# Moving the operand sums of x and u through the routing rounds of a spectral + PEER kernel (1 core)

## The chip, the cores and the metric

One core of one Trainium2 chip runs the kernel. The metric is the device time of one execution in microseconds (us): the median of three runs, each of which is the slowest core's time (there is one core here).

## The reference

For 2048 tokens of width 512, `y = x + FNet(xn) + PEER(xn)`, where `xn` is the layer norm of `x`:

```python
y = einsum("ts,bse->bte", re_s, xn @ re_d.T) - einsum("ts,bse->bte", im_s, xn @ im_d.T)   # real part of a 2-D DFT
q = einsum("nd,dhc->nhc", xf, w_q)             # 32 heads, two halves of 128
s1, s2 = q[..., :128] . k1, q[..., 128:] . k2  # 64 scores each; the best two of each half
cand = t1[..., :, None] + t2[..., None, :]     # 4 candidates of which the best two remain, out of 4096 experts
g = softmax(top_s)
act = gelu(einsum("nd,nhkd->nhk", xf, u[top_e]))
out = einsum("nhk,nhk,nhkd->nd", g, act, v[top_e])
```

The kernel doesn't gather experts: it computes `x @ u.T` for all 4096 of them, multiplies by the gates that the routing gives, and multiplies the product by `v`.

## The kernel before, in words

**Start (0 to about 96 us).** Loads, the layer norm, the transforms of the spectral part.

**Routing (to about 480 us).** Eight rounds `j` of four heads each, over 16 token tiles `i`; "tile n" below is number `16*j + i`. For each tile `scores` lets PE do 12 matmuls of 128x512 into one of four PSUM banks (L252), ACT copy the bank to one of four buffers `ss` (L949), and DVE find the best two per head (eight MAX8, L953, two FIND_INDEX8, L957). A bank comes free when ACT has copied it. A round's weights `m` are made during the round before: `m_prep` scales the raw weights (ACT L162; the scaled raw copy on ACT, L164, for parts t = 2 and 3, on POOL, L166, for t = 0 and 1) and takes the difference (POOL, L167), and `m_mul` multiplies them on PE (L148). `routing` turns the best two of each half into gates, early in the next round (lines 882 to 922, on POOL, DVE and ACT; L887 on POOL is what ACT's L890 takes). `y_rows` (PE L528 to L531, POOL L540 and L541) finishes rows of the spectral part during rounds 0 to 2.

Other work is spread among the tiles by `todo[n]`, a list of pieces for each tile, and each is tied to its tile by `behind()` (L737): ACT copies the piece's scale factor into a spare column of the tile's `ss` buffer, and the piece reads it from there. So a piece can't start before that `ss` buffer is in use for tile n. The pieces are:

- `fill_uv` (ACT L780 and L781, POOL L782): splits a block of `u` or `v` into two f16 halves in SBUF, 16 blocks of u and 9 of v.
- `sum_u`: for the eight blocks of u that belong to QUADS, four sums on POOL (L808 to L811), then `split4`, ACT's f16 copy of them (L794), POOL's difference (L795), and two stores to DRAM (`s_d`, L798).
- `sum_x`: the same for the six token pairs in PAIRS: one large sum (POOL L821), four small ones (L826 to L829), the same `split4`, two stores to `t_d` (L798). Its pieces stand at `todo[62 + 7n]` and just behind, but nothing in them is tied to the tile: `sum_x` takes no scale factor.
- `stage_v` (ACT L846 and L847, POOL L849): as a fill, but stored to DRAM.

All `sum_u` share one scratch buffer (`v_sb[8]`) and half of `v_sb[6]`, all `sum_x` share `v_sb[5]`, `v_sb[7]` and the other half of `v_sb[6]`; each next one waits until the store of the last has read them. A scheduler reorders the queue of each engine as data allow, so that the six `sum_x` without a tie stand in POOL's queue ahead of work of round 0.

**Products (from about 480 us).** PE computes `z = x @ u.T`, ACT takes gelu, PE expands the gates (L1241), DVE multiplies, PE multiplies by v (L1286). For six pairs of token tiles the products with the eight QUADS blocks follow a Strassen-like scheme (`z_pair`): seven products per quad (`slot`, L1153, 24 matmuls of 128x128), four of them with summed u (`s_d`, loaded at L1136 into a ring of three buffers) and some with summed x (`t_d`). `SEQ` gives the order: a digit is a product, a and b are the two quads, c is an ordinary block (24 matmuls of 128x256, L1092) out of PLAIN, the eight blocks outside QUADS. Products 5, 6, 3 and 7 read the ring; when one has been issued, `ring_load` refills its buffer. Gate expansions (L1241) are put between by a count of PE cycles done. The gelu of a quad writes its four blocks with a stride that `dst` gives.

Of the kernel before, what the change touches and what calls it, by code (L numbers as in the profile page):

```python
# [20 lines left out]
D = 512  # L21
# [7 lines left out]
XS = 512.0  # L29
V1 = 5  # L30
V2 = 9
QUADS = (0, 1, 2, 3), (8, 9, 10, 11)
PAIRS = tuple(range(2, 14, 2))


# [1 line left out]
def tile_fnet_peer(ctx, tc, x, ca, cb, c5, wt, wf, wr, wq, kt, ut, vn, out):  # L37
# [117 lines left out]
    def m_prep(j, t, pool, at):  # L155

        raw = MS[j, t].rearrange("p h k -> p (h k)")
        MS[j, t, "h"] = pool.tile([P, 2, D], F16, tag="wh", name=f"wh{j}_{t}", bufs=4)
        h = MS[j, t, "h"].rearrange("p h k -> p (h k)")
        l = raw.bitcast(F16)[:, 0:2 * D]  # L160
        MS[j, t, "l"] = l.rearrange("p (h k) -> p h k", h=2)
        nc.scalar.activation(h, raw, AF.Copy, scale=at)  # L162
        if t > 1:
            nc.scalar.activation(raw, raw, AF.Copy, scale=at)  # L164
        else:
            nc.gpsimd.tensor_scalar(raw, raw, sw, None, op0=ALU.mult)  # L166
        nc.gpsimd.tensor_tensor(l, raw, h, op=ALU.subtract)  # L167
# [553 lines left out]
    def part_b(safe, stS, stP, stQ, stE, xt, u_sb, cmp_p, w4):  # L721
# [11 lines left out]
        def behind(src, at):  # L733

            if at is None:
                return src
            nc.scalar.activation(at, src, AF.Copy)  # L737
            return at
# [48 lines left out]
        def scratch(g):  # L787
            return v_sb[g].rearrange("p l c d -> p (l c d)").bitcast(F32)
# [24 lines left out]
            split4(part - 1, s4, v_sb[6].rearrange("p l c d -> p (l c d)")[:, 0:2 * D],  # L813
                   lambda i: s_d[qd].rearrange("o p (t l f) -> t l p o f", t=4, l=2)[t, i])

        def sum_x(b, part):

            f, t4 = scratch(5), scratch(7)
            if part == 0:
                v = xq[b // 2]  # L820
                nc.gpsimd.tensor_tensor(f.rearrange("p (q f) -> p q f", q=2),  # L821
                                        v[:, :, 0].rearrange("p q k n -> p q (k n)"),
                                        v[:, :, 1].rearrange("p q k n -> p q (k n)"), op=ALU.add)
                b11, b21, b12, b22 = [f[:, k * 256:k * 256 + 256] for k in range(4)]
                r = [t4[:, k * 256:k * 256 + 256] for k in range(4)]
                nc.gpsimd.tensor_tensor(r[0], b12, b11, op=ALU.subtract)  # L826
                nc.gpsimd.tensor_tensor(r[1], b22, r[0], op=ALU.subtract)
                nc.gpsimd.tensor_tensor(r[2], b22, b12, op=ALU.subtract)
                nc.gpsimd.tensor_tensor(r[3], b21, r[1], op=ALU.subtract)  # L829
                return  # L830
            split4(part - 1, t4, v_sb[6].rearrange("p l c d -> p (l c d)")[:, 2 * D:],
                   lambda i: t_d[b // 2, :, i * 2 * D:i * 2 * D + 2 * D])

        SRAW = {}
# [139 lines left out]
        else:  # L974
# [8 lines left out]
            for j in range(2, NCH):  # L983
                for t in range(4):
                    todo[(j - 1) * NT + 2 * t - (12 if j == 2 else 4)].append(
                        lambda at, j=j, t=t: m_prep(j, t, wqp, behind(sw, at)))
        fills = [(0, g) for g in (0, 1, 2, 3, 8, 9, 10, 11, 12, 13, 14, 4, 5, 6, 7, 15)] + [(1, g) for g in range(V2)]
        slots = [29, 31, 36, 43, 45] + [16 * j + i for j in range(3, 7) for i in (4, 6, 11, 13)]
        slots += [113 + 2 * n for n in range(len(fills) - len(slots))]
        assert fills[slots.index(113)] == (1, V1)  # L990
# [3 lines left out]
            if which == 0 and not safe and any(g in q for q in QUADS):  # L994
                todo[n + 1].append(lambda at, g=g: (sum_u(g, 1), sum_u(g, 2)))
        if not safe:
            for n, b in enumerate(PAIRS):
                for part, at in enumerate((0, 2, 3)):
                    todo[62 + 7 * n + at].append(lambda at, b=b, part=part: sum_x(b, part))
        for g, n in zip(range(V2, 16), (25, 38, 41, 57, 73, 89, 105)):  # L1000
            todo[n].append(lambda at, g=g: stage_v(g, at, False))
            todo[n - 3].append(lambda at, g=g: fill_load(1, g))
# [98 lines left out]
        if not safe:  # L1101
            sx = stE.enter_context(tc.tile_pool(name="sx", bufs=1, side="left"))
            x4 = sx.tile([P, 2, 4, 2, P], F16, name="x4")
            PLAIN = [g for g in range(16) if not any(g in q for q in QUADS)]
            SEQ = ["c", "1a", "2a", "5a", "c", "6a", "3a", "c", "7a", "c", "4a", "1b", "2b", "5b", "c", "6b", "3b", "c",
                   "7b", "c", "4b", "c"]
            OPS = {"1": (0, None, None, 0), "2": (1, None, None, 1), "5": (None, 0, 0, None), "6": (None, 1, 1, None),
                   "3": (None, 3, None, 3), "7": (None, 2, 2, None), "4": (3, None, 3, None)}

# [50 lines left out]
        def z_pair(b, n, after):  # L1160

            cgs = iter(PLAIN)
            st = {}
            total, done, cg = sum(2616 if o == "c" else 1344 for o in SEQ), 0, 0
            for o in SEQ:
                if o == "c":
                    u_part(b, next(cgs))
                    done += 2616
                else:
                    op, qd = o[0], ("ab".index(o[1]) + n) % 2  # L1170
                    quad = QUADS[qd]

                    def dst(a, c):
                        return ACT[b[c]][:, 2 * quad[0] + a:2 * quad[3] + 2:2, :]

                    def v(p):
                        return p.rearrange("p (t n) -> p t n", t=4)

                    def gelu(d, src=None):
                        nc.scalar.activation(d, d if src is None else src, AF.Gelu_apprx_tanh, scale=zsc)  # L1180

                    if op in "125":
                        st["X" if op == "1" else "Y" if op == "2" else "Z"] = take(f"z{op}_{b[0]}_{qd}")
                    (X, Xt), (Y, Yt), (Z, Zt) = [st.get(k, (None, None)) for k in "XYZ"]
                    slot(op, quad, Z if op in "53" else Y if op == "2" else X, qd)
                    if op == "1":
                        nc.scalar.activation(dst(0, 0), v(X), AF.Copy)
                    elif op == "2":
                        nc.vector.tensor_tensor(dst(0, 0), v(Y), dst(0, 0), op=ALU.add)
                        banks.append(Yt)  # L1190
                    elif op == "5":
                        nc.scalar.activation(dst(1, 0), v(Z), AF.Copy)
                    elif op == "6":
                        nc.scalar.activation(dst(0, 1), v(X), AF.Copy)
                        gelu(dst(0, 0))
                    elif op == "3":
                        nc.vector.tensor_tensor(dst(0, 1), v(Z), dst(0, 1), op=ALU.add)
                        banks.append(Zt)
                    elif op == "7":
                        nc.scalar.activation(dst(1, 1), v(X), AF.Copy)  # L1200
                        nc.vector.tensor_tensor(dst(1, 1), dst(1, 1), dst(1, 0), op=ALU.add)
                        gelu(dst(0, 1))
                    else:
                        gelu(dst(1, 0), v(X))
                        gelu(dst(1, 1))
                        banks.append(Xt)
                    done += 1344
                while cg < 16 and done * 16 >= (cg + 1) * total:
                    after(cg)
                    cg += 1  # L1210
# [542 lines left out]
```

## Time and profile before

| | before |
|---|---|
| median of 3 runs | 1215.04 us (1213.74 to 1217.06) |
| the profiled execution | 1216.34 us |
| its span | 1214.2 us |
| busy: PE, DVE, ACT, POOL | 1142.1, 949.1, 631.6, 328.2 us |
| mean granted clock of TensorE | 0.976 |

The span is what the profiler shows from the first to the last instruction; 2.1 us of the execution lie around it. A row of the timeline reads: start, duration, engine, line, operation, output<-input, shapes, and in brackets how long the engine had been idle and on what it waited. A row of the waits reads: engine, what it was to do, what it waited for, total us, how often, the longest. A row of the windows is one stretch: busy us of each engine, with the number of instructions, then the granted TensorE clock as a share of full speed, and the DMA engines' share and rate. A row of a line's group has count, then the shortest, median and longest duration in ns, and the first and last start.

### The profile page before, as it was taken

The numbers are of one execution on the slowest core, as the hardware profiler recorded it, in microseconds if no ns is written. First come the engines' busy times: TensorE is split into PE (matmuls) and PEld (weight loads), VectorE is DVE, ScalarE is ACT, GpSimd is POOL, SyncE is SP. The second block draws the span as 40 slices with busy tenths as digits, with TensorE's granted clock in tenths as the row PEclk, the third lists the DMA queues.
The fourth block names the chain that finished last, engine by engine and source line by source line (L and its number), as shares of the span: only waits on it lengthen the run. The fifth ranks groups of instructions, "written<-read, shape, count | busy, mean of one in ns | idle before, by whom it ended". The sixth has DMA issues, their size and how long they took to land.

```text
span 1214.2 us, 27275 instructions
## 1 busy us (share of the span) xinstructions
PE 1142.1 (94%) x10748; PEld 731.7 (60%) x10748; DVE 949.1 (78%) x2855; ACT 631.6 (52%) x1061; POOL 328.2 (27%) x341
## 2 busy tenths in 40 slices
PE   9998496988999999998999999999999999999997
PEld 6454253443444545967847747748748748749663
DVE  7896465867799899996597787788888788888760
ACT  6664356747687673535443644644644644633440
POOL 1439579787775641000000000000000000000000
PEclk8998798998999999999999999999999999999999
DMA  9882335525233120537274585575575575461422
GB/s 296 274 233 104 128 106 164 176 79 165 96 122 140 45 96 11 179 114 251 76 257 161 178 260 166 184 258 171 174 252 170 178 252 189 168 205 47 147 79 99
DMA packets 114135, 195.73 MB, mean 161 GB/s; under 512 B 33988, under 2 KB 57419, under 8 KB 113998
## 3 DMA queue, kind: packets, MB, share of 16 engines
q1 hardware_dynamic: 113696, 193.83, 49.2%
q8 instruction: 86, 1.41, 0.5%
q14 instruction: 51, 0.42, 0.1%
q10 hardware_dynamic: 302, 0.08, 0.0%
HBM read 163.13 MB, written 24.97 MB: 155 GB/s over the span
## 4 chain that ended last, share of the span: by engine, by line
PE 59%; POOL 13%; DVE 13%; DMA 6%; ACT 5%; issue 3%; SPq 0%; POOLq 0%; ACTq 0%
PE v L1286 26%; PE z L1092 14%; PE z L1153 8%; PE s L252 4%; DVE vals L953 4%; PE g L1241 4%; DMA s<-s_d 3%; DVE idx L957 3%; PE p L449 2%; POOL w L167 2%; POOL w L166 2%; POOL u L782 2%; PE m L152 1%; POOL v L795 1%; DMA t_d<-v 1%
## 5 line engine op out<-in xcount | busy, mean ns | idle before, releaser
L252 PE MATMUL s<-m,xq 128*128 128x512 f16 x1344 | 308.9, 388 | 15.6 <-ACT ss L949 15.6
L252 PEld LDWEIGHTS <-xq 128*128 128x128 f16 x1344 | 132.3, 100 | 176.1 <-issue 33.0
L1286 PE MATMUL v<-v,act 128*128 128x512 f16 x1056 | 233.2, 379 | 0.0
L1092 PE MATMUL z<-xb,u 128*128 128x128 f16 (+1 forms) x2688 | 222.8, 243 | 0.0
L1092 PEld LDWEIGHTS <-u 128*128 128x128 f16 x2688 | 196.9, 98 | 13.3 <-issue 0.2
L1299 POOL TENSOR_TENSOR y<-y,xr 128x512 f32<-128x512 f32 x15 | 27.9, 1858 | 616.3 <-DMA y<-y_d 277.6
L1231 DVE TENSOR_TENSOR L<-io_lam,cmp 128x2048 f16<-128x2048 f16 x128 | 157.3, 1229 | 42.0 <-PE g L1241 42.0
L1286 PEld LDWEIGHTS <-act 128*128 128x128 f16 x1056 | 101.3, 98 | 117.7
L953 DVE MAX8 vals<-ss 128x8 f32<-128x64 f32 x896 | 133.6, 216 | 34.1 <-ACT ss L949 34.1
L1286 PE MATMUL v<-v,w 128*128 128x512 f16 x480 | 106.2, 379 | 0.0
L1362 ACT ACTIVATE cx<-cx 128x896 f32<-128x896 f32 x64 | 60.5, 945 | 66.8 <-DVE cx L1342 48.6
L957 DVE FIND_INDEX8 idx<-vals,ss 128x8 uint16<-128x256 f32 x224 | 93.8, 419 | 0.0
L949 ACT ACTIVATE ss<-s,wsc 128x512 f32<-128x512 f32 x120 | 78.3, 676 | 13.5 <-DVE idx L957 8.8
L1099 ACT ACTIVATE act<-z,scl 128x256 f32<-128x256 f32 (+1 forms) x88 | 44.2, 524 | 74.4 <-PE z L1092 74.4
L1256 ACT ACTIVATE act<-w 128x1024 f16<-128x1024 f32 x36 | 48.3, 1357 | 60.4 <-DVE w L1249 60.0
L1286 PEld LDWEIGHTS <-w 128*128 128x128 f16 x480 | 46.0, 98 | 53.4
L1153 PEld LDWEIGHTS <-s 128*128 128x128 f16 x1080 | 61.9, 98 | 16.6 <-DMA s<-s_d 16.4
L1336 DVE TENSOR_TENSOR cx<-cx 128x512 f32<-128x512 f32 (+2 forms) x84 | 48.6, 610 | 28.6 <-DMA cx<-in_cb_dram 28.6
L1241 PEld LDWEIGHTS <-L 128*128 128x128 f16 x2048 | 61.2, 96 | 11.5 <-DVE R L1239 1.2
L1249 DVE SCALAR_TENSOR_TENSOR w<-act,scl,g 128x1024 f32<-128x1024 f32 x44 | 55.9, 1280 | 11.1 <-ACT act L1099 11.1
L1257 DVE TENSOR_TENSOR act<-w,act 128x1024 f16<-128x1024 f32 x44 | 60.4, 1377 | 3.7 <-ACT act L1256 3.7
L1241 PE MATMUL g<-R,L 128*128 128x32 f16 x2048 | 62.7, 177 | 0.5 <-DVE R L1239 0.4
(362 smaller groups left out, 1733.2 us busy)
## 6 DMA issues: line engine op xcount, KB each, us to landing
v<-v_d SPq DMA_DIRECT2D x67, 512.0 KB, 4.1
cx<-in_cb_dram SPq DMA_DIRECT2D x64, 448.0 KB, 5.0
s<-s_d SPq DMA_DIRECT2D x30, 512.0 KB, 4.2
w<-in_wq_dram SPq DMA_DIRECT2D x28, 512.0 KB, 4.4
fit<-in_wq_dram SPq DMA_DIRECT2D x28, 512.0 KB, 5.8
uv<-in_vn_dram SPq DMA_DIRECT2D x16, 512.0 KB, 3.8
uv<-in_ut_dram SPq DMA_DIRECT2D x16, 512.0 KB, 4.1
c<-in_ca_dram SPq DMA_DIRECT2D x8, 512.0 KB, 4.8
```

The costliest lines, as they stand in the source:

```text
L252: nc.tensor.matmul(ps, xt[i][:, l, kd, :], m[:, r, kd, :], start=(n == 0), stop=(n == 3 * KD - 1))
L949: nc.scalar.activation(s, ps, AF.Copy, scale=inv)
L953: nc.vector.max(vals[:, i, w, :, h], s[:, g, :])
L957: nc.vector.max_index(idx[:, i, w].rearrange("p k h -> p (k h)"), vals[:, i, w, 0:2].rearrange("p k h -> p (k h)"), s[:, w * HC:g + 1, :]. ...
L1092: nc.tensor.matmul(ps if n == 1 else ps.rearrange("p (b n) -> p b n", b=2), ug[:, l, c % 2, kd, :], xb2[:, k0, r, kd, :] if n == 1 else xb ...
L1153: nc.tensor.matmul(bank[:, t * P:(t + 1) * P], lt, rt, start=(t == k == 0 and op in "125"), stop=(t == 3 and k == 5), skip_group_check=op ...
L1231: nc.vector.tensor_tensor(L.rearrange("p t (l two) -> p t l two", two=2), io_lam.rearrange("p (l two) -> p l two", two=2).unsqueeze(1).to_ ...
L1241: nc.tensor.matmul(p[:, hf, t * NC:(t + 1) * NC], L[:, t, :], R[:, t, :], start=True, stop=True)
L1249: nc.vector.scalar_tensor_tensor(w, act[:, :, ts], fw, p.rearrange("p h (n c) -> p c (h n)", c=NC), op0=ALU.mult, op1=ALU.mult)
L1257: nc.vector.tensor_tensor(w16[..., 1], w, w16[..., 0], op=ALU.subtract)
L1286: nc.tensor.matmul(pv, w16[:, c, :, l], v_sb[g][:, r, cc, :], start=(n + cc == 0 and k == 0), stop=(n == 15 and cc == 1 and k == 2))
L1362: later.append(lambda: nc.scalar.activation(tf[:, P:], tf[:, P:], AF.Abs, accum_out=chk[:, n:n + 1]))
```

## The change

Five edits:

1. `QUADS` becomes every second block from 8 up, and every second from 9 up (before 0 to 3 and 8 to 11); PLAIN is then 0 to 7 (before 4 to 7 and 12 to 15), and the stride in `dst` follows.
2. In `m_prep`, for the rounds j = 3 to 7, the scaled raw copy of part t = 1 is made by ACT (L164) and no longer by POOL (L166).
3. `sum_x` begins with a POOL copy of one column out of the tile's `ss` buffer, which ties it to a tile: 19, 21, 23, 25, 38 and 48, with its split two tiles on. It uses four pairs of scratch buffers in turn, `v_sb[0]` to `v_sb[7]`, and puts the f16 copy over its own sum, so `v_sb[6]` is no longer shared.
4. The fills of u and v are interleaved: the eight `sum_u` were at tiles 29, 31, 36, 43, 45, 52, 54 and 59; now they are at 43, 52, 61, 68, 77, 84, 93 and 100.
5. `SEQ` takes the parts in the same order for both quads and puts an ordinary block behind each product that reads the ring.

```diff
-QUADS = (0, 1, 2, 3), (8, 9, 10, 11)
+QUADS = (8, 10, 12, 14), (9, 11, 13, 15)
...
-        if t > 1:
+        if t > (1 if j == 2 else 0):
             nc.scalar.activation(raw, raw, AF.Copy, scale=at)
         else:
             nc.gpsimd.tensor_scalar(raw, raw, sw, None, op0=ALU.mult)
...
-        def sum_x(b, part):
-
-            f, t4 = scratch(5), scratch(7)
+        def sum_x(b, part, at=None):
+
+            n = PAIRS.index(b) % 4
+            f, t4 = scratch(2 * n), scratch(2 * n + 1)
             if part == 0:
                 v = xq[b // 2]
+                nc.gpsimd.tensor_copy(f[:, 0:1], behind(one, at))
...
-            split4(part - 1, t4, v_sb[6].rearrange("p l c d -> p (l c d)")[:, 2 * D:],
+            split4(part - 1, t4, f.bitcast(F16)[:, 0:2 * D],
...
-        fills = [(0, g) for g in (0, 1, 2, 3, 8, 9, 10, 11, 12, 13, 14, 4, 5, 6, 7, 15)] + [(1, g) for g in range(V2)]
+        fills = [divmod(n, 16) for n in (0, 1, 2, 8, 3, 10, 16, 4, 12, 14, 17, 5, 9, 11, 18, 6, 13, 15, 19, 7, 20,
+                                         21, 22, 23, 24)]
...
-            for n, b in enumerate(PAIRS):
-                for part, at in enumerate((0, 2, 3)):
-                    todo[62 + 7 * n + at].append(lambda at, b=b, part=part: sum_x(b, part))
+            for n, b in zip((19, 21, 23, 25, 38, 48), PAIRS):
+                todo[n].append(lambda at, b=b: sum_x(b, 0, at))
+                todo[n + 2].append(lambda at, b=b: (sum_x(b, 1), sum_x(b, 2)))
...
-            SEQ = ["c", "1a", "2a", "5a", "c", "6a", "3a", "c", "7a", "c", "4a", "1b", "2b", "5b", "c", "6b", "3b", "c",
-                   "7b", "c", "4b", "c"]
+            SEQ = [o if o == "c" else o + q for q in "ab" for o in "152c6c3c7c4"]
...
-                        return ACT[b[c]][:, 2 * quad[0] + a:2 * quad[3] + 2:2, :]
+                        return ACT[b[c]][:, 2 * quad[0] + a:2 * quad[3] + 2:2 * (quad[1] - quad[0]), :]
```

POOL's queue of the kernel before, towards the end of round 0 (`w_126` is raw weights for round 2, `v_920`, `v_921` and `v_922` are the scratch buffers of `sum_x`, `xq` is x):

```order
L407 TENSOR_TENSOR s5i<-r_1_640 1x127
L821 TENSOR_TENSOR v_920<-xq_104 128x1024
L826 TENSOR_TENSOR v_922<-v_920 128x256
L828 TENSOR_TENSOR v_922<-v_920 128x256
L827 TENSOR_TENSOR v_922<-v_920,v_922 128x256
L829 TENSOR_TENSOR v_922<-v_920,v_922 128x256
L821 TENSOR_TENSOR v_920<-xq_105 128x1024
L166 TENSOR_SCALAR w_126<-w_126,wsc 128x1024
L167 TENSOR_TENSOR w_126<-w_126,wh_0_888 128x1024
L166 TENSOR_SCALAR w_126<-w_126,wsc 128x1024
L795 TENSOR_TENSOR v_922<-v_922,v_921 128x1024
```

The same place in the changed kernel, where lines from `sum_x` on have numbers higher by two (`u_132` is a row of the spectral part):

```order
L407 TENSOR_TENSOR s5i<-r_1_640 1x127
L166 TENSOR_SCALAR w_126<-w_126,wsc 128x1024
L167 TENSOR_TENSOR w_126<-w_126,wh_0_888 128x1024
L166 TENSOR_SCALAR w_126<-w_126,wsc 128x1024
L167 TENSOR_TENSOR w_126<-w_126,wh_1_925 128x1024
L167 TENSOR_TENSOR w_126<-w_126,wh_2_965 128x1024
L167 TENSOR_TENSOR w_126<-w_126,wh_3_1033 128x1024
L540 TENSOR_TENSOR u_132<-u_132 1x127
L540 TENSOR_TENSOR u_132<-u_132 1x128
```

The sums of x have gone from between the weights of round 2. They stand further down, in round 1, behind the routing of round 0 (`lc`, `di` and `g` are its last results; `ss_3_1388` and `ss_5_1507` are the buffers of tiles 19 and 21):

```order
L924 CAST z<-lc_0_1356 128x16x2x4 x2
L924 CAST z<-di_0_1348 128x16x2x4 x2
L822 COPY v_915<-ss_3_1388 128x1
L895 TENSOR_TENSOR g_0_1486<-c_0_1308,g_0_1486 128x16x4
L823 TENSOR_TENSOR v_915<-xq_104 128x1024
L828 TENSOR_TENSOR v_916<-v_915 128x256
L830 TENSOR_TENSOR v_916<-v_915 128x256
L829 TENSOR_TENSOR v_916<-v_915,v_916 128x256
L831 TENSOR_TENSOR v_916<-v_915,v_916 128x256
L795 TENSOR_TENSOR v_916<-v_916,v_915 128x1024
L822 COPY v_917<-ss_5_1507 128x1
L823 TENSOR_TENSOR v_917<-xq_105 128x1024
```

Each sum of x is now in one piece there, with its L795 in front of the next one's copy.

ACT's queue of the kernel before, from the first gate of round 0 on (`uvpFalse` is the scale of u and v, from which PE's bank comes free):

```order
L890 ACTIVATE c_0_1308<-c_0_1306 128x64
L949 ACTIVATE ss_2_1330<-s_2_1317,wsc 128x512
L122 ACTIVATE uvpFalse<-uvs 128x2
L794 ACTIVATE v_921<-v_922 128x1024
L949 ACTIVATE ss_3_1388<-s_3_1375,wsc 128x512
L949 ACTIVATE ss_4_1442<-s_4_1429,wsc 128x512
L794 ACTIVATE v_921<-v_922 128x1024
L949 ACTIVATE ss_5_1500<-s_5_1487,wsc 128x512
L949 ACTIVATE ss_6_1550<-s_6_1537,wsc 128x512
L794 ACTIVATE v_921<-v_922 128x1024
```

The same place in the changed kernel:

```order
L892 ACTIVATE c_0_1308<-c_0_1306 128x64
L951 ACTIVATE ss_2_1330<-s_2_1317,wsc 128x512
L122 ACTIVATE uvpFalse<-uvs 128x2
L737 ACTIVATE ss_3_1388<-one 128x1
L951 ACTIVATE ss_3_1388<-s_3_1375,wsc 128x512
L794 ACTIVATE v_915<-v_916 128x1024
L951 ACTIVATE ss_4_1449<-s_4_1436,wsc 128x512
L737 ACTIVATE ss_5_1507<-one 128x1
L794 ACTIVATE v_917<-v_918 128x1024
L951 ACTIVATE ss_5_1507<-s_5_1494,wsc 128x512
L951 ACTIVATE ss_6_1568<-s_6_1555,wsc 128x512
L737 ACTIVATE ss_7_1596<-one 128x1
```

There the copies L737 are new, and ACT has an L794 of a sum of x between the evictions of tiles 19 to 22 (L951) as before, but out of a buffer that is its own.

## The prediction, on record before the changed kernel ran

> **What bounds the kernel now.** I read the page by slices first, then the routing rounds as windows, then the waits, then the timeline at the places that the windows point to. In the page's slices (tenths of busy time, 30 us each) the two rows that matter are:
>
> ```profile
> PE   9998496988999999998999999999999999999997
> ...
> POOL 1439579787775641000000000000000000000000
> ```
>
> PE is the engine that is nearly always busy, and has its holes only where POOL is full (slices 4 to 11). The windows below start at 103.40 us, and from 148.09 on each is one round, cut at the cast L894 by which a round's gates are finished:
>
> ```profile
> 103.40:148.09 44.69, 22.11 (x134) 11.70 (x133) 18.44 (x100) 21.44 (x57) 33.31 (x52) 0.73 0.24 80
> 148.09:212.71 64.62, 54.15 (x354) 28.30 (x353) 42.22 (x230) 38.89 (x77) 53.89 (x63) 0.92 0.46 145
> 212.71:266.45 53.74, 50.30 (x299) 23.53 (x298) 36.34 (x187) 35.29 (x51) 41.99 (x41) 0.93 0.46 142
> 266.45:322.95 56.50, 48.32 (x290) 22.36 (x289) 41.33 (x209) 35.55 (x52) 44.12 (x42) 0.94 0.37 112
> ...
> 367.27:411.58 44.31, 44.31 (x290) 21.56 (x288) 41.03 (x210) 32.95 (x49) 29.34 (x27) 1.00 0.32 108
> ```
>
> After the length come busy us of PE, PE's weight load, DVE, ACT and POOL, then the granted clock. A round is done in 44.31 us where PE never pauses (the last row); that is the floor. The three before it take 64.62, 53.74 and 56.50, with POOL at 42 to 54. So PE waits there, and the waits say for whom:
>
> ```profile
> ACT v L794 <- POOL v L811: 42.1, 8, 8.7
> ...
> ACT c L890 <- POOL c L887: 33.0, 6, 12.8
> ...
> ACT v L794 <- POOL v L829: 29.4, 4, 12.4
> ...
> PE s L252 <- ACT ss L949: 22.6, 16, 5.5
> ...
> PE m L148 <- ACT uvpFalse L122: 17.6, 1, 17.6
> ```
>
> POOL holds ACT (the split L794 of the sums, the gates L890), and ACT, whose queue is in order, holds the bank copies L949 and the scale L122 that PE needs. The worst place in the timeline:
>
> ```profile
> 108.44 5.28 PE L252 MATMUL s<-m,xb 128*128 128x512 f16 x12 [4.96 <-ACT ss L949]
> ...
> 118.12 2.75 PE L252 MATMUL s<-m,xq 128*128 128x512 f16 x12
> ...
> 141.39 0.27 PE L148 MATMUL m<-sums,wh 128*128 128x64 f16 x2 [17.62 <-ACT uvpFalse L122]
> ```
>
> ```profile
> 133.09 0.72 POOL L826 TENSOR_TENSOR v<-v 128x256 f32<-128x256 f32 x1 [10.14 <-DMA t_d<-v]
> ```
>
> ```profile
> 105.52 1.06 ACT L794 ACTIVATE v<-v 128x1024 f16<-128x1024 f32 x1 [12.44 <-POOL v L829]
> ...
> 140.45 0.26 ACT L890 ACTIVATE c<-c 128x64 f32<-128x64 f32 x1 [12.77 <-POOL c L887]
> ```
>
> POOL stands 10.14 us before the third sum of x, whose scratch the store to `t_d` still reads; round 0's gates are behind it on POOL, so ACT stands 12.77 us at L890, L122 comes after that, and PE stands 17.62 us.
>
> **What is at stake.** First window: 4.96 + 17.62, and a tile of 5.28 instead of 2.75 behind the first, 2.53: 25.1. Second: 64.62 − 44.31 = 20.3, of which the rows of the spectral part, four PE pieces in that round, are real work:
>
> ```profile
> 172.26 0.39 PE L528 MATMUL hy<-u,u 128*128 128x129 f32 x2
> ...
> 173.15 2.75 PE L252 MATMUL s<-m,xq 128*128 128x512 f16 x12
> ```
>
> 4 × (173.15 − 172.26) = 3.6, so 16.7 remain. Third: 9.4; fourth: 12.2. Together 63.4 us that PE could save in routing, 5% of the span.
>
> **The change part by part.** The durations it moves:
>
> ```profile
> L821 POOL TENSOR_TENSOR v<-xq x6: 2113/2124/2132, 79.0 to 153.4; 128x1024 f32<-128x1024 f16 x6
> ```
>
> ```profile
> L829 POOL TENSOR_TENSOR v<-v,v x6: 722/722/728, 83.3 to 161.7; 128x256 f32<-128x256 f32 x6
> ```
>
> ```profile
> L795 POOL TENSOR_TENSOR v<-v,v x14: 2123/2130/2147, 94.1 to 303.2; 128x1024 f16<-128x1024 f32 x14
> ```
>
> ```profile
> L794 ACT ACTIVATE v<-v x14: 1042/1057/1057, 84.5 to 298.2; 128x1024 f16<-128x1024 f32 x14
> ```
>
> ```profile
> L166 POOL TENSOR_SCALAR w<-w,wsc x12: 2841/2846/2855, 86.3 to 396.0; 128x1024 f32<-128x1024 f32 x12
> ```
>
> ```profile
> L167 POOL TENSOR_TENSOR w<-w,wh x24: 2112/2130/2137, 89.2 to 411.5; 128x1024 f16<-128x1024 f32 x24
> ```
>
> ```profile
> L164 ACT ACTIVATE w<-w,ss x12: 1132/1142/1149, 87.1 to 405.5; 128x1024 f32<-128x1024 f32 x12
> ```
>
> ```profile
> 138.11 0.32 POOL L884 TENSOR_TENSOR c<-u 128x64 f32<-128x64 f32 x1
> 138.39 0.88 POOL L540 TENSOR_TENSOR u<-u 128x127 f32<-128x127 f32 x2
> ```
>
> ```profile
> 116.07 0.19 ACT L737 ACTIVATE ss<-one 128x1 f32<-128x1 f32 x1
> ```
>
> One sum of x is 2.12 + 4 × 0.8 (0.72 and its gap) on POOL, 1.06 on ACT, 2.13 on POOL: a chain of 8.5 us, 7.5 of it POOL's. A sum of u is 4 × 0.73 + 2.13 = 5.05 on POOL and 1.06 on ACT.
>
> *Sums of x out of round 0 (edit 3).* The order shows POOL going from L407 straight to L166 and L167, then the rows and round 0's gates. The 10.14 us wait goes: four scratch pairs leave no earlier store to wait for among the first four. Then L887 is no longer late and both PE waits go. What is next there is ACT, with 21.44 us of work in that window beside PE's 22.11; I leave 3 us to it (25.1 − 3). **First window: −22.**
>
> *Sums of x in the second window.* Four chains, 4 × 8.5 + 1 = 35 us, tied to every second tile (5.5 us) from tile 19 on, so POOL falls behind by 3 us a sum. Behind them in POOL's queue stand a weight part of a coming round (2.85 + 2.13), three L167 (6.4), four rows of the spectral part at 1.75 (four pieces, two of them 0.88), round 1's gates (13 pieces of about 0.32, 4.3) and the fill's 2.13: 2 + 35 + 5.0 + 6.4 + 7.0 + 4.3 + 2.1 = 62 us after the window's start until the L167 that PE's L148 needs behind tile 37 is done (the first tie comes at 2), and PE would be there at 2 + 18 × 2.77 (44.31 / 16) + 3.6 = 55.4. So PE still waits about 6.4 us there, and with a slow tile behind it 8. **Second window: 16.7 becomes 8, −9.**
>
> *Third and fourth window.* Six sums of u (30 us of POOL) shrink to three (tiles 43, 52, 61), two sums of x come (15), one L166 of 2.85 goes in each. Single pieces with gaps of 9 tiles leave POOL time to catch up: I leave 5 and 1.5 us. **9.4 + 12.2 becomes 6.5, −15.**
>
> *Fifth to seventh window.* They are without a wait now, and get five sums of u: two a round bring POOL to 29.3 + 2 × 5.05 − 2.85 = 36.6 and ACT to 33 + 2 × 1.06 + 1.14 = 36.3 of 44.3. Neither becomes the bound, but each L794 can hold ACT up to the 8.7 us of the waits' row, 5.3 on average, against four banks of 2.77 us. **+3**, and +2 for the four sums of x whose L794 stands before an eviction.
>
> *Edit 2* takes 5 × 2.85 = 14.2 us from POOL for 5 × 1.14 = 5.7 on ACT; its worth is inside the windows above. *The copies* L737 (0.19 us, six of them) and POOL's one-column copies are covered by the same queues, 6 × 0.2 = 1.2 without cover. *The stride* of `dst` changes no count: nothing.
>
> *The pair phase (edits 1 and 5).* PE's wait there is for the ring:
>
> ```profile
> PE z L1153 <- DMA s<-s_d: 14.6, 10, 3.7
> ```
>
> ```profile
> s<-s_d SPq DMA_DIRECT2D x30, 512.0 KB, 4.2
> ```
>
> ```profile
> 656.21 2.78 PE L1092 MATMUL z<-xb,u 128*128 128x256 f16 x24
> 658.83 1.50 PE L1153 MATMUL z<-x,s 128*128 128x128 f16 x24
> ```
>
> ```profile
> L1241 PE MATMUL g<-R,L 128*128 128x32 f16 x2048 | 62.7, 177 | 0.5 <-DVE R L1239 0.4
> ```
>
> A load lands in 4.2 us in the middle. Before, an ordinary block (658.83 − 656.21 = 2.62) and a product (1.50) stand between freeing and use for product 3, 4.1 us; now a gate expansion (32 matmuls, 62.7 / 2048 × 32 = 1.0) and a block, 3.6. For product 7 it is as before. In the first half the two loads no longer fall together, and 3.7 us may shrink. Ends: 12 uses at −0.6 or +1 each, −7 to +7 with the first; the 14.6 us can't fall below nothing. **I take −3**, since two blocks now stand around each ring use instead of one.
>
> Sum: −22 − 9 − 15 + 3 + 2 − 3 = −44. Against the profiled execution (1216.34 = span 1214.2 + 2.1) that is 1172; the median of the runs lies 1.3 lower, 1215.04 − 44 = **1171**.
>
> **Two rules weighed.** The cast L894 shows that POOL and DVE get in each other's way:
>
> ```profile
> 148.09 0.21 DVE L894 CAST z<-g 128x128 f16<-128x128 f32 x1
> ...
> 367.27 2.13 DVE L894 CAST z<-g 128x128 f16<-128x128 f32 x1 [0.50 <-POOL g L893]
> ```
>
> With POOL idle it takes 0.21 us, beside POOL's work 2.13. DVE has 44.3 − 41.0 = 3.3 us left in a steady round; POOL's share there goes from 66% to 83%, so of some ten such instructions a round about two more are hit, 2 × 1.92 = 3.8 us: 0.5 a round more than there is, +2 over four rounds, inside the range. The Trainium skill, GPSIMD Engine Reference, section 8 "Key points", says that GpSimd shares its SBUF interfaces with VectorE and contends with DVE's 2-port modes and two-input instructions; the trace agrees as far as this cast shows, and by that rule this change, which moves POOL work into rounds where DVE is nearly full, costs.
>
> Behind a wait a tile is slow: 5.28 behind 4.96 us, where one without a wait takes 2.75; the windows' granted clock is 0.73 in the first, 0.92 to 0.94 in the next three and 1.00 when PE never waits. Slow tiles are some 13 us of the 63, and go with the waits. The Trainium skill, TensorE: Matmul & The Clock Gate, Part 1, "The HAM clock gate", has the clock drop after about 3.4 us of idling; by it waits below that would cost only themselves, which the sum doesn't need.
>
> **The rivals.**
>
> A. *POOL's heap passes on in full.* The four sums in a row put POOL 12 us behind in the second window; if this reaches PE by the banks as well as by L148, that window keeps 18 and not 8, and the third 10 and not 5: 1171 + 15 = **1186**. For it: before, POOL's 53.89 of 64.62 was what made that window the longest. Against: the third window's share of sums of u is gone.
>
> B. *All waits go*: routing falls by all 63 and the ring's 14.6 goes: 1215 − 63 − 14.6 = **1137**; with half of the ring 1145. For it: POOL's total over the first four windows falls by some 30 us, well below PE's. Against: the four chains in a row.
>
> C. *Slower: ACT passes its waits to PE one for one.* The fourteen L794 waited 42.1 + 29.4 = 71.5 us in twelve waits, 6 each; spread through rounds where PE now has no pause, 14 × 6 = 84 us replace the 63: 1215 − 63 + 84 = **1236**. It decides if over three quarters (63/84) passes. Before, 22.6 of 71.5 reached PE at L252, a third, since four banks cover 11 us.
>
> D. *The tie does nothing*, the scheduler keeps the old order: **1215**. The order above speaks against it.
>
> **How the numbers follow.** Forecast (1155 to 1182) 0.62, A (1182 to 1205) 0.17, B (below 1155) 0.14, C 0.04, D 0.03. Leaving out C, D and the outer parts of A and B gives 1147 to 1195. A measurement of this kernel tells 0.3% (3.6 us) from no change. Faster: forecast, A and B, 0.93. Same: D, 0.03. Slower: C, 0.04.
>
> **What would show it.** Right: no 10 us wait of POOL on `t_d`; PE's 17.6 us wait gone, 103 to 148 shorter by 22; second window about 53 us with one PE wait on L167 of some 6 us at its end; rounds five to seven at 45 us and not 44.3; ring waits about 11 us. Wrong: a round five to seven above 48 (C), a second window still above 60 (A), a first window still above 35 (ACT or DVE was the cause there), ring waits above 20.

## The result and the profile after

The changed kernel takes 1184.3 us (median of six runs, 1181.91 to 1187.3) against 1214.94 for the kernel before on the same chips: a ratio of 0.9745, 95% interval 0.9718 to 0.9771. That is 31 us faster; 44 were forecast. The profiled execution has a span of 1185.2 us, 29.0 less than before.

The page's slices, 29.6 us each, show PE without its deep holes, and a 6 in POOL's fourth slice where there was a 9:

```profile
PE   9999998889999999999999999999999999999997
...
POOL 1426897978768440100000010000000000000000
```

The same windows as in the prediction, cut at the cast of the gates (L896 now), the first from the same work on. Columns as there: length, busy us of PE, PE's weight load, DVE, ACT and POOL, granted clock, DMA:

```profile
103.10:125.25 22.15, 21.06 (x173) 12.35 (x173) 21.25 (x120) 14.07 (x38) 16.14 (x36) 1.00 0.18 59
125.25:181.41 56.16, 50.10 (x322) 25.99 (x321) 35.25 (x189) 41.16 (x83) 50.53 (x61) 0.97 0.51 172
181.41:238.79 57.38, 49.92 (x312) 23.80 (x310) 46.62 (x220) 36.22 (x53) 46.65 (x45) 1.00 0.38 125
238.79:285.81 47.02, 43.88 (x275) 20.98 (x276) 38.67 (x201) 35.43 (x51) 35.51 (x36) 0.96 0.47 154
285.81:333.64 47.83, 45.00 (x285) 21.51 (x283) 41.15 (x209) 35.66 (x52) 36.32 (x36) 0.96 0.41 133
333.64:381.48 47.84, 45.80 (x295) 22.16 (x293) 41.17 (x209) 35.67 (x52) 36.33 (x36) 1.00 0.34 111
```

The first window went from 44.69 to 22.15. The second is 8.5 shorter, the third 3.6 longer, the fourth 9.5 shorter, and the two steady rounds (the rows from 285.81 on) are 3.5 longer each, with POOL up from 29.34 to 36.3 and ACT from 32.95 to 35.7. The waits that answer to those of before:

```profile
ACT v L794 <- POOL v L811: 43.0, 8, 8.1
...
ACT v L794 <- POOL v L831: 28.5, 6, 6.9
...
PE s L252 <- ACT ss L951: 18.7, 13, 3.1
```

ACT still stands at the split L794 as long as before (71.5 us then, 71.5 now), though the sums are spread. PE's 17.6 us wait for the scale L122 is down to one of 1.09:

```profile
117.42 0.22 PE L148 MATMUL m<-sums,wh 128*128 128x64 f16 x2 [1.09 <-ACT uvpFalse L122]
...
180.06 0.20 PE L148 MATMUL m<-sums,w 128*128 128x64 f16 x1 [2.36 <-POOL w L167]
```

Where ACT's stand comes from is seen in a steady round. First ACT's queue, then POOL's, then PE's:

```profile
292.89 1.06 ACT L794 ACTIVATE v<-v 128x1024 f16<-128x1024 f32 x1 [6.82 <-POOL v L811]
293.85 0.67 ACT L951 ACTIVATE ss<-s,wsc 128x512 f32<-128x512 f32 x1
```

```profile
285.73 2.13 POOL L167 TENSOR_TENSOR w<-w,wh 128x1024 f16<-128x1024 f32 x1
287.81 2.13 POOL L782 TENSOR_TENSOR u<-uv,u 128x1024 f16<-128x1024 f32 x1
289.90 0.77 POOL L808 TENSOR_TENSOR v<-uv 128x256 f32<-128x256 f32 x1
...
292.13 0.72 POOL L811 TENSOR_TENSOR v<-uv,v 128x256 f32<-128x256 f32 x1
```

```profile
294.57 5.73 PE L252 MATMUL s<-m,xq 128*128 128x512 f16 x18 [2.83 <-ACT ss L951]
```

ACT has scaled the fill and goes straight to the split of its sum. POOL needs 7.1 us from 285.73 on to get there (a weight part, the fill's difference, four sums). All that time the bank copy L951 stands behind L794 on ACT; four banks cover most of it, PE waits 2.83 us, and the 18 matmuls behind the wait take 5.73 us, where 18 at the usual rate (12 in 2.6) take 3.9.

For the experiments one table is used. It is worked out from the traces: the first of the twelve matmuls L252 of each tile gives the tile's start, and the columns are the us from one tile's start to another's, up to the first product z, and the products to the end of the span. Sixteen tiles without a wait take 44.2.

```
tiles           0-16 16-20 20-36 36-52 52-68 68-84 84-100 100-116 116-z products
before          84.9  33.9  51.1  62.1  55.9  47.6  44.3   43.6   33.1   734.2
after           79.8  14.2  53.7  51.3  53.5  49.0  46.6   48.3   31.1   733.7
edit 3 alone    79.8  14.3  58.1  68.8  61.8  47.6  44.3   43.6   33.1   733.4
without edit 3  84.8  33.9  49.5  44.5  45.3  47.8  47.8   47.1   31.1   734.4
without 1, 4    79.8  14.3  57.3  66.4  60.7  44.2  44.2   43.5   31.1   733.8
without edit 2  79.9  14.4  53.4  53.5  59.1  52.4  50.8   46.1   31.1   726.0
without edit 5  79.8  14.3  53.6  51.3  53.5  49.0  46.6   48.3   31.1   734.6
u splits later  79.7  14.2  53.6  51.7  50.9  44.2  44.2   43.5   32.1   728.8
u, x splits     79.8  14.3  47.8  52.4  47.4  44.8  44.6   43.9   31.9   731.8
same, x spread  80.3  14.2  47.8  54.5  50.6  44.2  44.2   43.8   33.1   730.2
```

### The profile page after: what moved, and what is told of

It reads as the page before. It is cut to its first block, busy times and chain, and to the rows that moved or that the text cites. A ratio compares the mean times of both kernels' runs of the same rounds, so it can differ in the third digit from the quotient of the medians.

```text
span 1185.2 us, 27301 instructions
## 1 busy us (share of the span) xinstructions
PE 1136.8 (96%) x10748; PEld 730.8 (62%) x10748; DVE 953.4 (80%) x2855; ACT 636.8 (54%) x1072; POOL 315.1 (27%) x342
## 4 chain that ended last, share of the span: by engine, by line
PE 62%; POOL 15%; DVE 11%; DMA 6%; issue 3%; ACT 2%; SPq 0%; POOLq 0%; DVEq 0%; ACTq 0%
PE v L1288 26%; PE z L1095 15%; PE z L1155 8%; PE s L252 7%; PE g L1243 3%; DMA s<-s_d 3%; POOL u L782 2%; POOL w L167 2%; POOL v L795 2%; DVE u L955 1%; DVE vals L955 1%; POOL w L166 1%; DVE idx L959 1%; DVE u L959 1%; POOL v L823 1%
## 5 line engine op out<-in xcount | busy, mean ns | idle before, releaser
L252 PE MATMUL s<-m,xq 128*128 128x512 f16 x1344 | 305.1, 385 | 18.2 <-ACT ss L951 18.2
L252 PEld LDWEIGHTS <-xq 128*128 128x128 f16 x1344 | 131.6, 99 | 175.7 <-issue 30.7
L951 ACT ACTIVATE ss<-s,wsc 128x512 f32<-128x512 f32 x120 | 79.5, 679 | 17.2 <-PE s L252 8.6
L1102 ACT ACTIVATE act<-z,scl 128x256 f32<-128x256 f32 (+1 forms) x88 | 44.3, 524 | 39.5 <-PE z L1095 39.2
```

Of the source, the lines that this page charges most:

```text
L252: nc.tensor.matmul(ps, xt[i][:, l, kd, :], m[:, r, kd, :], start=(n == 0), stop=(n == 3 * KD - 1))
L951: nc.scalar.activation(s, ps, AF.Copy, scale=inv)
```

## The experiments

The theory: PE loses time in two ways. The sums of x ahead of round 0's gates on POOL cost the stretch up to tile 20; and each split that ACT reaches before POOL has made the sum holds the bank copies. The rival: POOL, or what it shares with DVE, is simply too full in these rounds.

**Edit 3 alone** (the kernel before, with the sums of x tied):

```diff
...
-            for n, b in enumerate(PAIRS):
-                for part, at in enumerate((0, 2, 3)):
-                    todo[62 + 7 * n + at].append(lambda at, b=b, part=part: sum_x(b, part))
+            for n, b in zip((19, 21, 23, 25, 38, 48), PAIRS):
+                todo[n].append(lambda at, b=b: sum_x(b, 0, at))
+                todo[n + 2].append(lambda at, b=b: (sum_x(b, 1), sum_x(b, 2)))
```

> The kernel before with edit 3 alone (sums of x tied to tiles 19 to 48, four scratch pairs); sums of u stay at tiles 29 to 59. Theory (POOL's sums of x ahead of round 0's gates were the first window's loss, and each split L794 that ACT reaches before POOL has summed costs PE about 3 us where PE has no other pause): the first window loses its 22 us, and the rounds up to tile 64 lose a little more than before, since four sums of x now stand ahead of the eight sums of u: 1190 to 1200 us. Rival (edit 3 is all of the gain, the new tiles of the sums of u are worth nothing): 1182 to 1187. Rival (the heap only moves): above 1207.

Measured: 1211.0 us, ratio 0.9961 (0.9942 to 0.998). The theory's number failed and the second rival's came true: the heap only moves. Up to tile 20 the table has 24.7 us less, from tile 20 to 68 it has 19.6 more. The waits of PE:

```profile
PE s L252 <- ACT ss L951: 29.5, 16, 4.0
...
PE m L148 <- POOL w L167: 8.1, 3, 5.2
```

Both are longer than before (22.6 and 5.7 us in that profile). Nearly everything that edit 3 gains in front is paid again behind.

**Without edit 3** (the changed kernel, with the old `sum_x`):

```diff
...
-            for n, b in zip((19, 21, 23, 25, 38, 48), PAIRS):
-                todo[n].append(lambda at, b=b: sum_x(b, 0, at))
-                todo[n + 2].append(lambda at, b=b: (sum_x(b, 1), sum_x(b, 2)))
+            for n, b in enumerate(PAIRS):
+                for part, at in enumerate((0, 2, 3)):
+                    todo[62 + 7 * n + at].append(lambda at, b=b, part=part: sum_x(b, part))
```

> The changed kernel with edit 3 undone: the sums of x without a tie, in one pair of scratch buffers. Theory (two separate losses: the sums of x ahead of round 0's gates cost the first window 22 us; the sums of u beside them in rounds 1 to 3 cost the rest): the first window's loss returns, of the heap in rounds 1 to 3 some 5 to 12 us go: 1193 to 1203 us. Rival (edit 4 works only together with edit 3, as edit 3 alone gave 5 us): 1209 to 1216.

Measured: 1191.77 us, ratio 0.9816 (0.9788 to 0.9844): the rival is out, and the time is just under the theory's 1193 to 1203, since more of the heap goes than the 5 to 12 us that the theory had. The long wait at the front is back,

```profile
PE m L148 <- ACT uvpFalse L122: 17.9, 1, 17.9
...
POOL v L826 <- DMA t_d<-v: 13.4, 3, 10.1
```

and tiles 36 to 68 run at the floor (44.5 and 45.3 us). So the sums of x are paid for behind even where the sums of u have moved. Most of the gain, 24 of 31 us, is there without the tie; edit 3 adds 5 us by the spans and 9 by the ratios (0.9816 to 0.9745): 24.7 in front, less the 19.2 that come back between tiles 20 and 68.

**Without edits 1 and 4** (sums of u at tiles 29 to 59 again). One form keeps the new QUADS and only puts their blocks first in the list of fills:

```diff
-        fills = [divmod(n, 16) for n in (0, 1, 2, 8, 3, 10, 16, 4, 12, 14, 17, 5, 9, 11, 18, 6, 13, 15, 19, 7, 20,
-                                         21, 22, 23, 24)]
+        fills = [(0, g) for g in (8, 10, 12, 14, 9, 11, 13, 15, 0, 1, 2, 3, 4, 5, 6, 7)] + [(1, g) for g in range(V2)]
```

> The changed kernel with edit 4 undone: the eight sums of u again stand at tiles 29, 31, 36, 43, 45, 52, 54 and 59 (blocks of the new QUADS). Theory: rounds 4 to 6 go back to 44.3 us each, 11 us less than in the changed kernel, and five more sums of u in rounds 1 to 3, which already hold six sums of x, cost 3 us each and some more by the heap, 15 to 25: 1188 to 1200 us. Rival (the early rounds have pauses of PE anyway, and only the rounds that were without a wait pay): 1172 to 1178.

Measured: 1199.66 us, ratio 0.9852 (0.982 to 0.9885). In this kernel the fills of blocks 8 and 10 write over factors of the spectral part that its rows at tiles 30 to 32 still read, so those rows come out with other values and the work there waits (71.7 us for tiles 20 to 36). The other form takes the old QUADS and the old list:

```diff
-QUADS = (8, 10, 12, 14), (9, 11, 13, 15)
+QUADS = (0, 1, 2, 3), (8, 9, 10, 11)
...
+        fills = [(0, g) for g in (0, 1, 2, 3, 8, 9, 10, 11, 12, 13, 14, 4, 5, 6, 7, 15)] + [(1, g) for g in range(V2)]
```

> The changed kernel with edits 1 and 4 undone: the old QUADS and the old list of fills, with the sums of u at tiles 29 to 59. Theory (the heap that edit 3 puts into round 1 is only worked off early if the sums of u stand later): rounds 4 to 6 at 44.3 us, but tiles 28 to 64 some 20 us longer than in the changed kernel: 1195 to 1204 us. Rival (it is the number of pieces in rounds 4 to 6 that counts): 1172 to 1180.

Measured: 1197.22 us, ratio 0.9855 (0.9827 to 0.9882). Tiles 68 to 116 are at the floor, 12 us better than in the changed kernel, and tiles 20 to 68 take 26 us more. Edit 4, with 1, is worth 13 us, and the rival, that only the steady rounds pay, is out.

**Without edit 2:**

```diff
-        if t > (1 if j == 2 else 0):
+        if t > 1:
```

> The changed kernel with edit 2 undone: five L166 of 2.85 us go back to POOL, five L164 of 1.14 leave ACT. Theory (PE pays when ACT stands before an L794 that waits for POOL, and each L166 that is ahead of a sum in POOL's queue makes that longer): 3 to 8 us longer than the changed kernel, 1187 to 1192. Rival (POOL has 11 us to spare in these rounds, so that it is hidden): 1182 to 1186.

Measured: 1196.51 us, ratio 0.9871 (0.9838 to 0.9904); the runs spread from 1190.3 to 1203.96, and the profiled one is the fastest. The effect has the theory's sign and about twice its size. In the profile the rounds from tile 36 on take 13 us more than in the changed kernel, and both rows of the theory grow:

```profile
ACT v L794 <- POOL v L811: 48.2, 8, 8.1
...
PE s L252 <- ACT ss L951: 33.4, 20, 5.0
```

18.7 us of PE's waits became 33.4. Why its products took 726.0 us in that profile, 7.7 less than in the changed kernel's, no run settles.

**Without edit 5:**

```diff
-            SEQ = [o if o == "c" else o + q for q in "ab" for o in "152c6c3c7c4"]
+            SEQ = ["c", "1a", "2a", "5a", "c", "6a", "3a", "c", "7a", "c", "4a", "1b", "2b", "5b", "c", "6b", "3b", "c",
+                   "7b", "c", "4b", "c"]
```

> The changed kernel with the old SEQ. The traces show the products 0.5 us shorter after the change. Theory (SEQ is worth nothing that a measurement tells): 1182 to 1187 us. Rival (the forecast's term of 3 us stands, and something else in the products took it back): 1187 to 1190, with more ring waits than the 9.1 us of the changed kernel.

Measured: 1186.36 us, ratio 0.9754 (0.9726 to 0.9783), which can't be told from the changed kernel's 0.9745. The ring's wait does what was forecast, and more; with the old order, then with the new:

```profile
PE z L1156 <- DMA s<-s_d: 14.3, 11, 3.8
```

```profile
PE z L1155 <- DMA s<-s_d: 9.1, 7, 2.4
```

Of the 5.2 us the products keep 0.9. One place where it goes is the last pair, where PE reaches a product before ACT's copy L1202 of an earlier one (part 7) has freed its bank:

```profile
988.44 1.50 PE L1155 MATMUL z<-x,s 128*128 128x128 f16 x24
...
994.73 2.18 PE L1155 MATMUL z<-x,u 128*128 128x128 f16 x24 [2.17 <-ACT act L1202]
996.71 2.49 PE L1155 MATMUL z<-xb,u 128*128 128x128 f16 x24
```

2.17 us of waiting and 0.68 + 0.99 us of slow matmuls behind it make 3.8.

**The splits later.** This tells the theory from its rival: POOL, DVE and ACT keep all their work in the same rounds, and only ACT's split is tied, three tiles later than it stood.

```diff
...
-                nc.scalar.activation(h, t, AF.Copy)
+                nc.scalar.activation(h, t, AF.Copy, scale=behind(one, at) if at is not None else 1.0)
...
-                todo[n + 1].append(lambda at, g=g: (sum_u(g, 1), sum_u(g, 2)))
+                todo[n + 4].append(lambda at, g=g: (sum_u(g, 1, at), sum_u(g, 2)))
```

> The changed kernel with the split L794 of each sum of u tied by a copy L737 to a tile three later; POOL's work, ACT's work and their rounds stay. Theory (PE pays because ACT stands 7 to 8 us before L794 with the bank copies L951 behind it, not because POOL or DVE is too full): the 2 to 5 us that rounds 4 to 6 lost each go, and about 3 us for each of the three earlier sums: 1164 to 1174 us. Rival (POOL's load, or its port with DVE, makes these rounds longer): no change, 1182 to 1187.

Measured: 1167.61 us (1167.28 to 1169.72), ratio 0.961 (0.9586 to 0.9635): 17 us faster than the changed kernel, in the theory's range. In the traces 13.4 us of this lie between tile 0 and the first product (427.6 became 414.2); the products are 4.9 us shorter too, though the edit doesn't touch them, and no run settles why. ACT, then POOL, at the same sum as above (it is at other times in this trace):

```profile
289.70 1.14 ACT L794 ACTIVATE v<-v,ss 128x1024 f16<-128x1024 f32 x1
```

```profile
285.25 0.73 POOL L811 TENSOR_TENSOR v<-uv,v 128x256 f32<-128x256 f32 x1
...
290.92 2.13 POOL L795 TENSOR_TENSOR v<-v,v 128x1024 f16<-128x1024 f32 x1 [0.94 <-ACT v L794]
```

The sum is ready 3.7 us before ACT comes to it, L794 has no wait, and tiles 68 to 116 take 44.2, 44.2 and 43.5 us. POOL's load was not the cause in these rounds: it is as high as in the changed kernel, and PE never pauses. A steady round, columns as above:

```profile
323.50:367.90 44.40, 44.40 (x290) 21.69 (x289) 40.97 (x209) 35.66 (x53) 36.17 (x35) 1.00 0.47 144
```

Tiles 20 to 68 keep nearly all they had (158.5 became 156.2). PE's row in the waits:

```profile
PE s L252 <- ACT ss L951: 10.0, 8, 3.1
```

**The splits of x later, too:**

```diff
...
-                todo[n + 2].append(lambda at, b=b: (sum_x(b, 1), sum_x(b, 2)))
+                todo[n + 4].append(lambda at, b=b: (sum_x(b, 1, at), sum_x(b, 2)))
```

> As the run in which the splits of the sums of u are tied three tiles later, with the splits of the sums of x tied two tiles later as well. Theory: PE's waits of 2.0, 1.6, 3.1 and 1.7 us behind the sums of x go: 1158 to 1164 us. Rival (the four sums in a row keep POOL itself late, so that PE then waits for L167 in place of L951): 1166 to 1170.

Measured: 1164.41 us (1158.72 to 1168.04), ratio 0.9585 (0.9556 to 0.9613). It is the fastest median of the study, 3 us under the run before, though the intervals overlap. Both expectations have a part: tiles 20 to 36 take 5.8 us less and 52 to 68 3.5 less, and ACT no longer waits at L794 at all, but PE now waits for POOL itself:

```profile
177.02 0.23 PE L148 MATMUL m<-sums,w 128*128 128x64 f16 x1 [4.86 <-POOL w L167]
```

**The first sums of x spread:**

```diff
-            for n, b in zip((19, 21, 23, 25, 38, 48), PAIRS):
+            for n, b in zip((19, 23, 27, 32, 40, 48), PAIRS):
```

> As the run with the splits of both kinds of sums tied later, with the first tiles of the sums of x at 19, 23, 27, 32, 40 and 48 instead of 19, 21, 23, 25, 38 and 48. Theory (what is left in round 1 is POOL late for L167 behind four sums in a row: one wait of 4.9 us and a slow tile behind it, tiles 36 to 40 at 20.7 us and not 12.5): 4 to 9 us less, 1155 to 1161 us. Rival (POOL's whole work up to that L167 counts, not where the sums stand, as all four still come before it): 1162 to 1167.

Measured: 1171.04 us (1166.3 to 1175.2), ratio 0.9633 (0.9606 to 0.966). It is above both ranges. The theory fell here: the wait grew,

```profile
177.36 0.23 PE L148 MATMUL m<-sums,w 128*128 128x64 f16 x1 [7.33 <-POOL w L167]
```

since POOL has all four sums ahead of that L167 either way, and in this form starts them later, the fourth at 169.9 us, right in front of it. In round 1 it is POOL's work up to that weight part that counts: there the rival holds.

**The kernel before, with only the splits of u later** (the same edit as in the run of that kind above):

> The kernel before with one edit: the split L794 of each sum of u tied three tiles later. The eight sums of u stay at tiles 29 to 59 and the sums of x where they were. Theory, first half (ACT's stand before L794 is what PE pays): rounds 1 to 3 lose part of their 38 us of waits, 1196 to 1206 us. Theory, second half (with one scratch buffer, sums 2 to 9 tiles apart now wait for each other's split and store, so that POOL stands before L808): the gain is taken back there, 1207 to 1220. Rival (POOL's load alone sets these rounds): 1213 to 1219 with no wait of POOL at L808.

Measured: 1212.5 us, ratio 0.9963 (0.9946 to 0.9981). Here three of the eight sums are written over by the next one before their split, so those parts of `s_d` hold other values; the work and its count stay, but these three don't wait for the sum before them, and the expectation's second half is tested only in part. One sum does stand as forecast, for the store of an earlier one:

```profile
235.24 0.74 POOL L808 TENSOR_TENSOR v<-uv 128x256 f32<-128x256 f32 x1 [4.50 <-DMA s_d<-v]
```

So the rival's sign, no wait there, isn't met. ACT's stand was halved, and PE's wait for the bank copies stayed as it was:

```profile
ACT v L794 <- POOL v L811: 22.0, 4, 12.2
...
PE s L252 <- ACT ss L949: 22.7, 12, 6.9
```

The longest stand of ACT, 12.2 us up to 248.16, is at the split of a sum that has been written over: it waits for the later sum too, whose last L811 ends at 248.13, and PE's longest wait for a bank, 6.9 us, follows. So the run shows that this edit alone gives no more than some 4 us in the kernel before, with its one scratch buffer; whether later splits would pay there with a buffer for each sum, no run shows.

## Why the prediction was right, and where it was off

The time, 1184.3 us, lies above the forecast's own 1155 to 1182, at the lower end of rival A's band and next to its 1186. That it is so near A's number is luck. A had 10 us left over the floor in the third window, which kept 13.1 (57.38 − 44.31, of which some 3 only because the cast comes later in its tile), but also 18 in the second, which kept 8.2 (56.16 − 44.3 − 3.6) as forecast; and it had no loss in the steady rounds beyond the forecast's 3 us.

- *First window, −22.* Right: 44.69 became 22.15, by the steps named (POOL has no wait for `t_d` any more, L122 is on time). By tiles it is 24.8 up to tile 20. Most of it is handed on: 19 of 24.7 us come back behind tile 20, as the run without edit 3 shows, and the forecast had such a heap in its second window alone.
- *Second window, −9.* Right: −8.5. The wait for L167 at its end is there, 2.36 us where some 6 were forecast (the row at 180.06).
- *Third and fourth window, −15.* This term failed, in size. The two together lie between the same tiles (38 and 71) before and after, and went from 110.2 to 104.4 us, −5.8. By tiles, 20 to 68 went from 169.1 to 158.5, −10.6, for −24 of the three windows. The forecast left waits of 8, 5 and 1.5 us there, counted from POOL being late for L167. It priced ACT's stand before the splits at 2 us for the sums of x, all in the second window, and at nothing for the sums of u in these windows, with single pieces that "leave POOL time to catch up". But POOL needs its time from the start of a piece to the sum, 7 us for u, whatever went before, and ACT is there at once. With the splits of u later, tiles 20 to 68 take 156.2, 2.3 less; with those of x later too 147.6, another 8.6 less. So most of what is missing is the term of 2 us for the sums of x, which measured 8.6 in this order of the two edits.
- *Tiles 68 on, +3.* The mechanism was right, the size wasn't. The five sums of u cost 12.0 us between tiles 68 and 116 (143.9, and 131.9 with their splits later), 4 times the forecast: in the row at 294.57 it is 2.83 us of wait and 1.8 of slow matmuls. By tiles this comes to +6.4 net (168.6 became 175.0), since 3.6 us of the old heap had reached behind tile 68 and 2.0 went between tile 116 and the products, which no run explains. It is rival C in small: ACT's waits of 71.5 us cost PE 20 us at the most (427.6 us from tile 0 to z became 407.0 with both splits later), under a third and far from the three quarters at which the change would have lost.
- *The pair phase, −3.* The ring's wait fell by 5.5 us (14.6 to 9.1), more than forecast, but the products by 0.5; a time within 3.6 us can't be told from none. Edit 2, to which the forecast gave no term of its own, turned out to be worth 12 to 15 us of the whole.
- *DVE beside POOL, +2 inside the range.* Not seen in the steady rounds: DVE's busy time went from 41.03 to 41.17 us though POOL's went up by 7. The cast L896 takes 2.13 us beside POOL's L167 (at 181.41) and 0.21 with POOL idle (at 125.25). The prediction's row of 0.21, at 148.09, is a weaker case: POOL's L795 ends and its L828 starts within it. The Trainium skill, GPSIMD Engine Reference, section 8 "Key points", names contention between GpSimd and VectorE over shared SBUF interfaces; the trace agrees as far as this cast shows. That a round holds too little of such work to count is the likely reason, and wasn't tested.

Sum by tiles: −24.8 − 10.6 + 6.4 − 0.5 = −29.5, and 0.4 that the start was later: −29.1, against −29.0 of the spans.

## What to carry to other kernels

Moving work off a crowded stretch moves its queue with it: ask who reads the moved result next, on which in-order engine, and what stands behind that reader. A piece that goes from one engine to a second and back (ACT, POOL, ACT) should have its last step tied later than its first by at least the second engine's time; that one edit, 17 us, 13 of them in the routing rounds, was worth as much here as the largest of the five. Test each edit by taking it away: edit 3, which closes the deepest hole of the profile, is worth 5 us alone and 5 to 9 in the whole, as most of its 24.7 us in front come back behind; edits 1 and 4 are worth 13, edit 2, which looked like a detail, 12 to 15, and edit 5 nothing that could be told.

## What the runs showed of the hardware

How long PE must idle for its matmuls to slow is not one number in these traces. In the changed kernel the matmuls behind a wait of 2.83 us were slow, and those behind 3.12 us weren't:

```profile
195.06 15.70 PE L252 MATMUL s<-m,xq 128*128 128x512 f16 x72 [3.12 <-ACT ss L951]
```

72 matmuls in 15.70 us are 2.6 us for twelve, full speed. The product behind 2.17 us in the last pair was slow again.

The granted clock in the record settles it. In the changed kernel it falls to half at 135.20, 241.01, 295.62, 391.20, 541.38 and 995.36 us, for 3.41 us each time, and these times lie whole multiples of 3.413 us apart (105.81 is 31 of them, 54.61 is 16). Cut by that grid, first the stretch in which the wait of 2.83 us lies and the one behind it, then the two over which the grid spreads the wait of 3.12 us and the one behind them (length, busy us of PE, PE's weight load, DVE, ACT and POOL, granted clock, DMA):

```profile
292.21:295.62 3.41, 1.04 (x5) 0.48 (x5) 3.34 (x23) 2.69 (x4) 2.25 (x2) 1.00 0.22 62
295.62:299.03 3.41, 3.41 (x9) 1.22 (x8) 3.38 (x22) 3.38 (x7) 2.51 (x2) 0.50 1.04 282
...
189.82:193.23 3.41, 2.12 (x10) 0.88 (x9) 3.34 (x23) 0.53 (x1) 3.25 (x5) 1.00 0.60 239
193.23:196.64 3.41, 1.58 (x8) 0.75 (x8) 1.88 (x12) 3.27 (x6) 3.41 (x3) 1.00 0.33 123
196.64:200.05 3.41, 3.41 (x18) 1.52 (x17) 3.41 (x17) 3.35 (x6) 0.87 (x1) 1.00 0.55 156
```

In the six stretches ahead of a fall PE was busy for 0.96 to 1.37 us; in no other stretch, from 60 us to the last matmul, for less than 1.54. So what counts in this trace is how long PE idles within one stretch of a fixed grid, not how long one wait is, and a wait that the grid cuts in two can be longer and slow nothing. The traces of the other runs have a grid of the same spacing, and their border lies between 1.9 and 2.1 us of idling in a stretch.

The Trainium skill, TensorE: Matmul & The Clock Gate, Part 1 "The HAM clock gate", has the clock fall after an idle window of about 3.4 us, in windows that run free of the program. The trace agrees with the length of the windows and with their running free; it doesn't agree that a whole window must be idle, as 2.04 of 3.41 us were enough. So the reading in the prediction that waits below 3.4 us cost only themselves doesn't hold here.
